# One 128-token tile of experts 1 to 7: w1's 128x128 chunks are held in TensorE and the tokens stream, where the tokens were held and w1 streamed

## The chip, the core and the metric

The kernel runs on one core of one Trainium2 chip. The metric is the time of one execution on the device in microseconds (us), taken as the median of several runs. TensorE (PE) multiplies: it loads a stationary operand of up to 128x128 (rows PEld in the trace) and streams a moving operand through it into PSUM. VectorE (DVE), ScalarE (ACT) and GpSimd (POOL) do the elementwise work; SyncE (SP) and POOL issue transfers.

## The reference, cut to what matters

Three stages follow one another: a block-causal attention over 4 x 8 heads of 576 positions, a dense feed-forward layer with a leaky ReLU, and a mixture of 8 experts. The change touches the last stage alone, and there the experts 1 to 7:

```python
def _moe2_ref(x, w_skip, w_gate, w1, w2):      # x: 2304 x 512, w1: 8 x 512 x 1024, w2: 8 x 1024 x 512
    do_compute = x @ w_skip > 0
    xc = x[do_compute]
    logits = xc @ w_gate
    e_idx = np.argmax(logits, axis=1)
    ...
    for e in range(E):
        mask = e_idx == e
        h = np.maximum(xc[mask] @ w1[e], 0.0)
        y[mask] = gate_w[mask, None] * (h @ w2[e])
    out[do_compute] = xc + y
```

## The kernel before, in words

Attention and the dense layer take the first 700 us or so. Routing then writes, for each expert, a list of its tokens. An expert works through its tokens in tiles of 128: a gather by index brings 128 rows of x, `turn_x` turns them on TensorE so that the 512 features lie on the partitions (four chunks of 128 features x 128 tokens, `xw`), and the tile function does the two products. Expert 0 uses `expert_tile`, which splits each operand in two parts and is not touched. Experts 1 to 7 use `expert_tile32`, in plain fp32; the trace shows each plain fp32 matmul as two records (two passes), each with a weight load of its own, and each transpose as one.

A tile of `expert_tile32` does this. `mm1(f, c)` makes the intermediate values of half f (512 of the 1024 columns) from feature chunk c: the tokens are the stationary operand, 512 columns of w1 move, and the result `ph[f]` has tokens on the partitions. `relu` copies it through ACT into `hs`. The second product needs the intermediate values with their own index on the partitions, so `turn_h` turns `hs` in four 128x128 transposes on TensorE, and DVE copies the result from PSUM into `hw`. `mm2(f)` then multiplies chunk f of `hw` with chunk f of w2 into `py`, eight chunks in a row. Late in the tile `ahead` puts in the `turn_x` of the next expert's first tile. At the end `finish` weighs `py` by the gate and adds x (DVE, L987), and POOL scatters the rows to the output (L988).

The order on TensorE is the order in which the code is written: each matmul is kept in program order. After an expert's first tile stands a branch (the `tc.If` at L1150): all engines read the count of the expert's tokens and jump over the code of the second to fourth tile and of a loop for more, if the count doesn't ask for them. In the names of the trace, `cv` is `xw`, `wbt` and `xT` are the buffers that hold w1 and w2, `raw` is `hw`, `pt` is a PSUM bank of transposes, `xg` and `xgf` are gathered rows, and q behind an engine's name is its sequencer. An expert's weights are loaded by SP (L847, L849) into one of four places, four experts ahead (expert 3's and 4's after expert 0).

Of the kernel before, what the change touches and what calls it, by code (L numbers as in the profile page):

```python
# [15 lines left out]
AF = mybir.ActivationFunctionType  # L16
# [9 lines left out]
def run_all(steps):  # L26
    for s in steps:
        s()
# [318 lines left out]
def attention_moe_kernel(  # L347
# [13 lines left out]
    nc = tc.nc  # L361
# [9 lines left out]
    ND = D // 128  # L371
    NF2 = F2 // 128
# [8 lines left out]
    ident = C.tile([128, 128], F32, name="ident")  # L381
# [535 lines left out]
    def places(own=False):  # L917

        bank = lambda nm, *shape: ps3.tile([128, *shape], F32, name=nm, tag="ps")
        return dict(hh=M3.tile([128, NF2, 128], F32R, name="hh", bufs=1),  # L920
                    hl=M3.tile([128, NF2, 128], F32R, name="hl", bufs=1),
                    ph=[bank("ph3", 512) for _ in range(2)],
                    py=psx.tile([128, 512], F32, name="py", bufs=1) if own else bank("py", 512),
                    pt=lambda: bank("pt", 4, 128), hs=lambda f: M3.tile([128, 512], F32, name="hs"),
                    yo=lambda: M3.tile([128, 512], F32, name="yo"))
# [58 lines left out]
    def finisher(lx, at, py):  # L984
        def finish():
            yo = at["yo"]()
            end = nc.vector.scalar_tensor_tensor(out=yo, in0=py, scalar=lx["li"][:, 2:3], in1=lx["xg"], op0=ALU.mult, op1=ALU.add)  # L987
            nc.gpsimd.indirect_dma_start(out=out[:, :], out_offset=bass.IndirectOffsetOnAxis(ap=lx["ix"][:, 1:2], axis=0),  # L988
                                         in_=yo, in_offset=None, bounds_check=NT - 1, oob_is_err=False)
            return end  # L990

        return finish

    def expert_tile32(e, hw, lx, ahead=(), at=None):

        a, b = weights[e]
        at = at or places()
        ph, py = at["ph"], at["py"]
        h = {}

        def mm1(f, c):
            tc.keep_in_program_order(nc.tensor.matmul(ph[f], lx["xw"][:, c], a[c][:, f * 512 : f * 512 + 512], start=(c == 0), stop=(c == ND - 1)))

        def mm2(f):
            tc.keep_in_program_order(nc.tensor.matmul(py, hw[:, f], b[f], start=(f == 0), stop=(f == NF2 - 1)))

        def relu(f):
            h[f] = at["hs"](f)
            nc.scalar.activation(out=h[f], in_=ph[f], func=AF.Relu)

        def turn_h(f):
            pt = at["pt"]()
            for c in range(4):
                tc.keep_in_program_order(nc.tensor.transpose(pt[:, c], h[f][:, c * 128 : (c + 1) * 128], ident))
            nc.vector.tensor_copy(hw[:, 4 * f : 4 * f + 4], pt)

        for c in range(ND):
            mm1(0, c)
        relu(0)
        for c in range(2):  # L1020
            mm1(1, c)
        turn_h(0)
        for c in range(2, ND):
            mm1(1, c)
        relu(1)
        for f in range(2):
            mm2(f)
        turn_h(1)
        for f in range(2, 6):
            mm2(f)  # L1030
        run_all(ahead)
        for f in range(6, NF2):
            mm2(f)
        return finisher(lx, at, py)
# [6 lines left out]
    for i in range(len(seq) + lag):  # L1041
# [11 lines left out]
        f = i - (len(seq) - NFB)  # L1053
# [16 lines left out]
        if i >= lag:  # L1070
            n, f = seq[i - lag]
# [54 lines left out]
    hw = [CV.tile([128, NF2, 128], F32, name="raw", bufs=3) for _ in range(2)]  # L1126
# [3 lines left out]
    for e in range(E):  # L1130
        ahead1 = [lambda: turn_x(firsts[e + 1])] if e + 1 < E else []
        some = ExitStack()
        if e:
            if e == E - 1:
                some.enter_context(tc.If(nreg[e] > 0))
            second = lane32(lall[1], e, xgs[4], xws[2])
            gather(second)
            finish = expert_tile32(e, hw[0], firsts[e], ahead1, at=places(True))

        def later(k_):  # L1140
# [3 lines left out]
            return (lane32 if e else lane)(L, n, xgs[4 + (k_ + 1) % 2], (xws if e else xts)[2 + (k_ + 1) % 2])  # L1144

        tile_of = (lambda *a: expert_tile32(e, hw[1], *a)) if e else expert_tile

        def more(k_, lx):
# [63 lines left out]
```

## Time and profile before

| | |
|---|---|
| median of 3 runs | 866.15 us (863.11 to 866.83) |
| the profiled execution | 863.9 us, span of the trace 862.1 us |
| PE busy | 795.8 us, 92% of the span |
| DVE, ACT, POOL busy | 518.6, 397.6, 352.3 us |
| experts 1 to 7 | from 739.8 us to the end |

The trace is of one execution; the span runs from its first instruction to its last. In a row of the timeline the first number is the start, the second how long the row lasts, and x12 says that twelve instructions are merged in it; behind it stands in brackets how long the engine had been idle and what it waited for. A matmul's record reaches past the start of the next one, since matmuls are pipelined, so a pace is read from starts.

### The profile page before, as it was taken

The page shows a single profiled execution, that of the slowest core. Times are in us where ns is not written, and L with a number is a line of the kernel's source. Part 1 is how long each engine was busy: PE and PEld are TensorE (multiplying, and loading weights), DVE is VectorE, ACT ScalarE, POOL GpSimd, SP SyncE. Part 2 cuts the span into 40 slices and gives each one's busy share as a digit, 9 for nine tenths or more (in the row PEclk, how much of TensorE's full clock was granted, in tenths as well). Part 3 has the DMA queues.
Part 4 walks back from the last instruction along what each step waited for, and adds up shares of the span by engine and source line. Part 5 has one row for each costly group of instructions (what it writes and reads, how often), then busy time and mean ns, then how long its engine had stood idle before and what let it go on. Part 6 is the DMA issues. An engine that isn't in the chain of part 4 may idle for free. (4 is left out here: it accounts for less than half of the span.)

```text
span 862.1 us, 12392 instructions
## 1 busy us (share of the span) xinstructions
PE 795.8 (92%) x4100; PEld 651.2 (76%) x4100; DVE 518.6 (60%) x1131; ACT 397.6 (46%) x909; POOL 352.3 (41%) x427
## 2 busy tenths in 40 slices
PE   6788999999999989799999999999999969989995
PEld 4577787989889788588999988798998758544442
DVE  6886788888878794776522799977222722111111
ACT  5887788887878774654422212222233312101010
POOL 3765554463545664654323234354225331010210
PEclk9799999999999999999999999999999989999998
DMA  6664753474332152652400663123126651693910
GB/s 164 173 169 100 203 108 94 102 202 118 77 100 56 39 183 82 217 198 74 147 1 16 205 184 110 36 76 111 65 103 207 236 85 37 240 396 134 326 60 7
DMA packets 114653, 112.89 MB, mean 131 GB/s; under 512 B 76718, under 2 KB 79790, under 8 KB 114562
## 3 DMA queue, kind: packets, MB, share of 16 engines
q1 hardware_dynamic: 106386, 95.72, 36.7%
q0 software_dynamic: 8176, 16.06, 6.2%
q8 instruction: 44, 0.72, 0.3%
q14 instruction: 47, 0.39, 0.1%
HBM read 81.23 MB, written 22.70 MB: 121 GB/s over the span
## 5 line engine op out<-in xcount | busy, mean ns | idle before, releaser
L447 PE MATMUL ph<-xT,wbt 128*128 128x384 f32 x864 | 166.8, 338 | 5.0 <-DVE u L438 2.7
L447 PEld LDWEIGHTS ph<-xT,wbt 128*128 128x128 f32 x864 | 152.0, 188 | 14.8 <-DVE u L438 5.0
L439 POOL TENSOR_TENSOR gl<-u,gh 128x384 fp32r<-128x384 f32 x72 | 79.7, 1107 | 155.2 <-ACT gh L438 147.2
L447 PE MATMUL acc<-wbt,gh 128*128 128x512 f32 x432 | 132.9, 396 | 0.0
L185 POOL TENSOR_SCALAR P<-P,stat 128x128 f32<-128x128 f32 (+2 forms) x144 | 79.1, 572 | 76.1 <-DVE stat L183 52.8
L438 DVE TENSOR_TENSOR u<-ph,u 128x384 f32<-128x384 f32 x72 | 39.7, 551 | 89.7 <-ACT u L437 89.7
L438 ACT CAST gh<-u 128x384 fp32r<-128x384 f32 x72 | 36.9, 513 | 121.0 <-DVE u L438 52.7
L447 PEld LDWEIGHTS acc<-wbt,gh 128*128 128x128 f32 x432 | 79.8, 188 | 12.3
L447 PE MATMUL acc<-wbt,gl 128*128 128x512 f32 x216 | 81.9, 395 | 0.0
L285 PE MATMUL pv<-ph,vs 128*128 128x320 f32 (+4 forms) x280 | 70.7, 323 | 2.7 <-DVE ph L239 1.6
L236 PE MATMUL pt<-ident,P 128*128 128x128 f32 x400 | 62.7, 283 | 6.7 <-ACT P L174 2.5
L437 ACT ACTIVATE u<-ph 128x384 f32<-128x384 f32 x72 | 35.2, 489 | 70.6 <-PE ph L447 66.8
L161 PE MATMUL sp<-wbt 128*128 128x128 f32 (+2 forms) x192 | 57.1, 376 | 9.6 <-DVE ph L239 2.8
L447 PE MATMUL ph<-xT,wia 128*128 128x384 f32 x288 | 59.0, 351 | 2.8 <-DVE cv L438 2.0
L447 PE MATMUL po<-woa,gA 128*128 128x512 f32 x216 | 56.2, 403 | 3.5 <-ACT gA L438 2.8
L285 PEld LDWEIGHTS pv<-ph,vs 128*128 128x128 f32 x280 | 51.3, 193 | 9.1 <-DVE ph L239 2.7
L418 POOL TENSOR_TENSOR cv<-cv,cv 128x512 int32<-128x512 int32 x32 | 43.7, 1367 | 33.8 <-DVE cv L417 21.7
L236 PEld LDWEIGHTS pt<-ident,P 128*128 128x128 f32 x400 | 47.1, 144 | 12.8 <-ACT P L174 3.0
L662 DVE CUSTOM_DVE_ANT_0 xlast<-x,raw 128x512 f32<-128x512 f32 x72 | 55.0, 803 | 0.0
L447 PEld LDWEIGHTS ph<-xT,wia 128*128 128x128 f32 x288 | 51.5, 195 | 4.3 <-DVE cv L438 2.5
L243 DVE TENSOR_TENSOR pl<-pt,ph 128x512 fp32r<-128x512 f32 (+2 forms) x84 | 50.9, 624 | 5.1 <-ACT ph L242 4.1
L447 PEld LDWEIGHTS po<-woa,gA 128*128 128x128 f32 x216 | 39.9, 191 | 13.1 <-ACT gA L438 3.7
(244 smaller groups left out, 1533.9 us busy)
## 6 DMA issues: line engine op xcount, KB each, us to landing
wbt<-in_moe_w_dram SPq DMA_DIRECT2D x48, 512.0 KB, 7.7
wbt<-wbt SPq DMA_DIRECT2D x60, 144.0 KB, 2.6
raw<-in_moe_w_in_dram SPq DMA_DIRECT2D x16, 512.0 KB, 4.1
raw<-in_moe_w_out_dram SPq DMA_DIRECT2D x16, 512.0 KB, 4.1
xTd<-xT POOLq DMA_DIRECT2D x4, 1152.0 KB, 8.0
part_d<-cv SPq DMA_DIRECT2D x18, 256.0 KB, 2.1
x<-part_d SPq DMA_DIRECT2D x6, 768.0 KB, 7.9
xT<-xTd POOLq DMA_DIRECT2D x6, 768.0 KB, 7.4
```

What stands on the lines that cost most here:

```text
L161: nc.tensor.matmul(o_, st()[a][h][:, rows : rows + m], st()[b][:, h, c : c + w], start=(i == 0), stop=(i == 1))
L185: nc.gpsimd.tensor_scalar(out=P, in0=P, scalar1=rs[:, i : i + 1], scalar2=1.0, op0=ALU.mult, op1=ALU.mult)
L236: nc.tensor.transpose(o, src, self.ident)
L243: nc.vector.tensor_tensor(out=dl, in0=s_, in1=dh.bitcast(F32), op=ALU.subtract)
L285: nc.tensor.matmul(box["pv"][:, c0:N], v, box[t][:, i, h, cs], start=(jc == 0 and t == "ph"), stop=(jc == runs[-1][0] and t == parts[-1]))
L418: nc.gpsimd.tensor_tensor(out=w, in0=w, in1=low, op=ALU.add)
L437: nc.scalar.activation(out=u, in_=ph, func=AF.Copy, scale=0.01)
L438: return [nc.vector.tensor_tensor(out=u, in0=ph, in1=u, op=ALU.max), nc.scalar.copy(gh, u), nc.gpsimd.tensor_tensor(out=gl, in0=u, in1=gh. ...
L439: nc.gpsimd.tensor_tensor(out=gl, in0=u, in1=gh.bitcast(F32), op=ALU.subtract)]
L447: nc.tensor.matmul(ps, x, y, start=first and m == 0, stop=last and m == 3 * n - 1)
L662: nc.vector.tensor_tensor_reduce(out=junk, in0=x2[:, t], in1=wrow[j], scale=1.0, scalar=0.0, op0=ALU.mult, op1=ALU.add, accum_out=box["L"] ...
```

## The change

The first product of a tile changes sides. The stationary operand is now a 128x128 chunk of w1 (feature chunk c, columns f*128 to f*128+127), and the 128 tokens of `xw` move. `mm1(f)` does four such matmuls for each of eight f, and leaves 128 intermediate values on the partitions and the tokens along the row; four f share one PSUM bank. `relu(i)` writes a whole bank into `hw` at once. `turn_h`, its transposes, the copies by DVE and the tile `hs` are gone. `mm2`, `ahead` and `finish` are as before.

```diff
-        def mm1(f, c):
-            tc.keep_in_program_order(nc.tensor.matmul(ph[f], lx["xw"][:, c], a[c][:, f * 512 : f * 512 + 512], start=(c == 0), stop=(c == ND - 1)))
+        def mm1(f):
+            for c in range(ND):
+                tc.keep_in_program_order(nc.tensor.matmul(
+                    ph[f // 4][:, f % 4 * 128 : f % 4 * 128 + 128], a[c][:, f * 128 : f * 128 + 128], lx["xw"][:, c],
+                    start=(c == 0), stop=(c == ND - 1)))
...
-        def relu(f):
-            h[f] = at["hs"](f)
-            nc.scalar.activation(out=h[f], in_=ph[f], func=AF.Relu)
-
-        def turn_h(f):
-            pt = at["pt"]()
-            for c in range(4):
-                tc.keep_in_program_order(nc.tensor.transpose(pt[:, c], h[f][:, c * 128 : (c + 1) * 128], ident))
-            nc.vector.tensor_copy(hw[:, 4 * f : 4 * f + 4], pt)
+        def relu(i):
+            nc.scalar.activation(out=hw[:, 4 * i : 4 * i + 4].rearrange("p f t -> p (f t)"), in_=ph[i], func=AF.Relu)
 
-        for c in range(ND):
-            mm1(0, c)
+        for f in range(4):
+            mm1(f)
         relu(0)
-        for c in range(2):
-            mm1(1, c)
-        turn_h(0)
-        for c in range(2, ND):
-            mm1(1, c)
+        for f in range(4, NF2):
+            mm1(f)
         relu(1)
-        for f in range(2):
-            mm2(f)
-        turn_h(1)
-        for f in range(2, 6):
+        for f in range(6):
             mm2(f)
         run_all(ahead)
```

On TensorE the code of a tile becomes this (expert 1's second tile stands for all; a row's xN counts matmuls as written, two passes each in fp32, one for a transpose):

```order
 L903 MATMUL pt<-ident,xgf_4228 128x128 x4
-L1002 MATMUL ph_7954<-wbt_7457,cv_7495 128x512 x4
-L1002 MATMUL ph_7955<-wbt_7457,cv_7495 128x512 x2
-L1014 MATMUL pt<-ident,hs 128x128 x4
-L1002 MATMUL ph_7955<-wbt_7457,cv_7495 128x512 x2
-L1005 MATMUL py<-wbt_7458,raw 128x512 x2
-L1014 MATMUL pt<-ident,hs 128x128 x4
-L1005 MATMUL py<-wbt_7458,raw 128x512 x4
+L1006 MATMUL ph_7964<-cv_7495,wbt_7457 128x128 x16
+L1006 MATMUL ph_7965<-cv_7495,wbt_7457 128x128 x16
+L1011 MATMUL py<-wbt_7458,raw 128x512 x6
 L903 MATMUL pt<-ident,xg_7488 128x128 x4
```

The eight transposes of L1014 are gone, and the eight matmuls of 512 columns have become 32 of 128; the first six of `mm2` follow without a break.

On DVE, at the same tile, the two copies of L1015 are gone and nothing takes their place; what stands around them keeps its order (L1143 is the branch that was L1150):

```order
-L1150 COMPARE_AND_BRANCH
-L906 COPY cv_7495<-pt 128x256
-L1015 COPY raw<-pt 128x512 x2
+L1143 COMPARE_AND_BRANCH
+L906 COPY cv_7495<-pt 128x256
 L906 COPY cv_7496<-pt 128x256
 L987 SCALAR_TENSOR_TENSOR yo<-py,la1li,xgf_4228 128x512
```

What moved on DVE is thus only the place of the branch in the queue, by two instructions. ACT keeps two activations in each tile, which now write `raw` and not `hs`. Ahead of expert 1 no engine's order changes.

## Rows read from the trace of the kernel before

**Rows 1.** The page: span, and granted clock in 40 slices.

```profile
span 862.1 us, 12392 instructions
...
PEclk9799999999999999999999999999999989999998
```

**Rows 2.** Busy time by window: two tiles (start:end, length, engines, clock, DMA, GB/s).

```profile
739.50:756.00 16.50, 15.29 (x44) 7.17 (x44) 3.01 (x5) 1.57 (x3) 2.00 (x2) 1.00 0.96 352
...
820.20:835.80 15.60, 15.30 (x45) 7.17 (x44) 2.56 (x4) 1.57 (x3) 1.96 (x2) 1.00 0.10 33
```

**Rows 3.** Timeline of PE, one whole tile (expert 5's) and the next one's start.

```profile
820.57 5.39 PE L1002 MATMUL ph<-wbt,cv 128*128 128x512 f32 x12 [0.30 <-PEq L1150]
825.80 0.60 PE L1014 MATMUL pt<-ident,hs 128*128 128x128 f32 x4
826.23 1.88 PE L1002 MATMUL ph<-wbt,cv 128*128 128x512 f32 x4
827.95 1.88 PE L1005 MATMUL py<-wbt,raw 128*128 128x512 f32 x4
829.67 0.60 PE L1014 MATMUL pt<-ident,hs 128*128 128x128 f32 x4
830.11 3.60 PE L1005 MATMUL py<-wbt,raw 128*128 128x512 f32 x8
833.54 0.60 PE L903 MATMUL pt<-ident,xg 128*128 128x128 f32 x4
833.98 1.88 PE L1005 MATMUL py<-wbt,raw 128*128 128x512 f32 x4
836.16 0.67 PE L1002 MATMUL ph<-wbt,cv 128*128 128x512 f32 x1 [0.30 <-PEq L1150]
```

**Rows 4.** Timeline of PE: the starts of the second and the fourth tile.

```profile
756.94 5.39 PE L1002 MATMUL ph<-wbt,cv 128*128 128x512 f32 x12 [1.84 <-PEq L1150]
...
789.40 5.39 PE L1002 MATMUL ph<-wbt,cv 128*128 128x512 f32 x12 [0.95 <-DVEq L1150]
```

**Rows 5.** Timeline of ACT and DVE in the tile of rows 3.

```profile
828.21 0.60 ACT L1009 ACTIVATE hs<-ph 128x512 f32<-128x512 f32 x1 [3.27 <-PE ph L1002]
...
830.30 0.69 DVE L1015 COPY raw<-pt 128x512 f32<-128x512 f32 x1 [3.18 <-PE pt L1014]
```

**Rows 6.** Timeline of PEld: fp32 loads, for 128 moving columns (attention) and for 9 (routing).

```profile
49.54 0.52 PEld L285 LDWEIGHTS pv<-ph,vs 128*128 128x128 f32 x4
49.98 0.19 PEld L161 LDWEIGHTS sp<-wbt 128*128 128x128 f32 x1
...
676.05 2.65 PEld L678 LDWEIGHTS lt<-wg,xlast 128*128 128x128 f32 x23
678.62 0.30 PEld L915 LDWEIGHTS eph<-wbt,xtf 128*128 128x128 f32 x2
```

**Rows 7.** Timeline of PE: the matmuls that belong to the first loads of rows 6.

```profile
49.55 0.71 PE L285 MATMUL pv<-ph,vs 128*128 128x128 f32 x4
50.01 0.42 PE L161 MATMUL sp<-wbt 128*128 128x384 f32 x1
```

**Rows 8.** Groups by form: one weight load of mm1 and of a transpose (busy, mean ns).

```profile
L1002 PEld LDWEIGHTS ph<-wbt,cv 128*128 128x128 f32 x96 | 17.3, 190 | 25.6 <-issue 24.9 <-ACT cv L905 0.7
...
L1014 PEld LDWEIGHTS pt<-ident,hs 128*128 128x128 f32 x56 | 7.0, 141 | 7.4 <-issue 7.1 <-ACT hs L1009 0.2
```

**Rows 9.** Timeline of SP: the loads of expert 6's weights.

```profile
788.57 1.76 SPq L847 DMA_DIRECT2D wbt<-in_moe_w_dram  x4
790.44 2.25 SPq L849 DMA_DIRECT2D wbt<-in_moe_w_dram  x4
```

**Rows 10.** Transfers from 739 us on: issues, KB each, median us from issue to landing.

```profile
wbt<-in_moe_w_dram SPq DMA_DIRECT2D x32, 512.0 KB, 8.3
```

**Rows 11.** Timeline behind the last tile: the weighing, and the scatter to the output.

```profile
851.49 0.75 DVE L987 SCALAR_TENSOR_TENSOR yo<-py,la0li,xg 128x512 f32<-128x512 f32 x1 [0.89 <-PE py L1005]
852.52 1.00 POOL L988 DMA_INDIRECT out_dram<-yo,la0ix  x1 [13.99 <-DVEq L1180]
```

More of the change, by code (lines that the diff above doesn't have):

```diff
@@ L998, in expert_tile32 @@
         ph, py = at["ph"], at["py"]
-        h = {}
-        def mm1(f, c):
-            tc.keep_in_program_order(nc.tensor.matmul(ph[f], lx["xw"][:, c], a[c][:, f * 512 : f * 512 + 512], start=(c == 0), stop=(c == ND - 1)))
+        def mm1(f):
[3 more added lines that the diff above has]
+                    start=(c == 0), stop=(c == ND - 1)))
         def mm2(f):
             tc.keep_in_program_order(nc.tensor.matmul(py, hw[:, f], b[f], start=(f == 0), stop=(f == NF2 - 1)))
-        def relu(f):
-            h[f] = at["hs"](f)
-            nc.scalar.activation(out=h[f], in_=ph[f], func=AF.Relu)
-        def turn_h(f):
-            pt = at["pt"]()
-            for c in range(4):
-                tc.keep_in_program_order(nc.tensor.transpose(pt[:, c], h[f][:, c * 128 : (c + 1) * 128], ident))
-            nc.vector.tensor_copy(hw[:, 4 * f : 4 * f + 4], pt)
-        for c in range(ND):
-            mm1(0, c)
-        relu(0)
-        for c in range(2):
-            mm1(1, c)
-        turn_h(0)
-        for c in range(2, ND):
-            mm1(1, c)
+        def relu(i):
+            nc.scalar.activation(out=hw[:, 4 * i : 4 * i + 4].rearrange("p f t -> p (f t)"), in_=ph[i], func=AF.Relu)
+        for f in range(4):
+            mm1(f)
+        relu(0)
+        for f in range(4, NF2):
+            mm1(f)
         relu(1)
-        for f in range(2):
-            mm2(f)
-        turn_h(1)
-        for f in range(2, 6):
+        for f in range(6):
             mm2(f)
```

## The prediction

> **What bounds the kernel now.** I read the page first. The span is 862.1 us and the clock row stands at 9 in nearly every slice, full speed, 2.4 GHz [rows 1]; the change touches only what comes after 739.8 us, so the next view was busy time by window there. In the window of expert 5's tile PE is busy 15.30 us of 15.60 at granted clock 1.00, while DVE has 2.56 us, ACT 1.57 and the DMA share is 0.10 [rows 2]. So in this stage TensorE alone sets the time, and whatever is taken from PE's own queue comes off the end. The timeline of PE then gives a tile piece by piece [rows 3]: three quarters of mm1 from 820.57, four transposes at 825.80, the rest of mm1, four passes of mm2, four transposes at 829.67, and so on; the next tile starts at 836.16, 15.59 us later. No PE row inside the tile has an idle time in brackets, so no wait inside it is there to be removed: the change can only gain what the transposes cost as work.
>
> The number of tiles comes from the groups: 56 loads of transposes of hs, eight in a tile, make seven tiles in this execution [rows 8].
>
> **What goes.** Eight transposes in each tile. In rows 3 four take from 825.80 to 826.23 and from 829.67 to 830.11, 0.43 and 0.44 us, so 0.87 us a tile and 6.1 us in seven tiles. DVE's copies (0.69 us each, [rows 5]) and the tile hs go too; they lay beside PE's work and are worth nothing by themselves.
>
> **What is added.** mm1 has the same number of multiplications but another form. Before: 16 passes of 512 columns; a pass takes (833.54 - 830.11)/8 = 0.429 us [rows 3], so 6.86 us. After: 64 passes of 128 columns, each with a weight load of its own. The streaming alone is a quarter of 0.429, 0.107 us, and would cost nothing more. The question is the load, for there are 64 now instead of 16. Before, a load (190 ns in its record, [rows 8]) lay behind 0.429 us of streaming; that cover is gone.
>
> The trace has this very shape elsewhere. In attention four fp32 loads for 128 moving columns start at 49.54 and the next one at 49.98 [rows 6]: 0.44/4 = 0.110 us for load and pass together. The matmuls that belong to them start at 49.55 and the next one at 50.01 [rows 7]: 0.115 us, the first one's start included. In the routing 23 fp32 loads for only 9 moving columns start at 676.05 and the next load at 678.62 [rows 6]: 2.57/23 = 0.112 us. With 9 columns there is hardly any streaming, so 0.112 us is the load itself; with 128 columns, 0.107 us of streaming, it is no slower. Load and stream lie beside each other, and the slower one, the load, sets the pace. I take 0.112 us, the longest series: 64 x 0.112 = 7.17 us, against 6.86 before, so 0.31 us more a tile.
>
> The Trainium skill speaks against the change here: "TensorE: Matmul & The Clock Gate", Part 3, section "The mechanism", says that a weight load overlaps matmuls in flight only when it goes to another group of rows of the array. All loads here fill all rows. By the row a pass costs 0.112 us; by that rule it would cost load and stream one after the other (a rival below). The two series just read, 9 and 128 columns at one pace, contradict it for fp32.
>
> **The sum.** Removed 0.87, added 0.31: 0.56 us a tile. Seven tiles give 3.9 us. The bounds of the pace: as low as 0.107 us if the load hid wholly behind the stream (then the 0.87 is kept nearly whole, 6.1 us in seven tiles), as high as the 0.115 us of rows 7 (64 x 0.115 = 7.36, 0.37 a tile, 2.6 us). Nearest is the long fp32 series, since each load here also follows another fp32 load without a break.
>
> **Waits that could come.** mm2(0) needs relu(0), which now writes hw itself. relu takes 0.60 us and used to start 0.26 us after mm1's last pass gave way to mm2 at 827.95 [rows 3, 5]; between the end of f = 3 and mm2(0) stand 32 passes of mm1, 3.6 us, so about 2.7 us are to spare. mm2(4) needs relu(1); behind mm1 come eight passes of mm2, 8 x 0.429 = 3.4 us, against 0.9. If that cover were gone, each of the two would cost its 0.9 us, and the gain would turn into a loss; nothing in the order takes it away. Weights: SP issues expert 6's last four loads at 790.44 to 792.69 [rows 9], they land 8.3 us after issue in the median [rows 10], and the tile that needs them starts at 836.16 [rows 3]. A stage that is 4 us shorter doesn't reach that. Behind the last tile DVE weighs from 851.49 and POOL scatters at 852.52 [rows 11]; that follows the last matmul as before and moves forward with it.
>
> The profiled execution took 863.9 us, 1.8 more than its span, and would take 863.9 - 3.9 = 860.0. The median of the three runs is 866.15, 2.25 above it; from the median I predict **862.2 us**, a ratio of 0.9955. I count 0.5% (4.3 us) as what a measurement of this kernel can tell from no change; the forecast lies just inside of it.
>
> **Rivals.**
> 1. *Less comes through, because code arrives late.* Between tiles PE branches over code that isn't needed. In rows 3 this leaves PE idle for 0.30 us on either side of the tile, put down to its own sequencer [rows 3], but ahead of the second tile it is 1.84 us, and ahead of the fourth 0.95 us, put down to DVE's sequencer [rows 4], in the time when weights stream in at a DMA share of 0.96 [rows 2]. A tile's PE code grows from 44 load-and-matmul pairs (32 passes and 12 transposes) to 84, and the code that is jumped over grows alike. If that wait ends at a moment that DMA traffic sets, a tile that ends 0.56 us earlier just waits longer. For it: the wait is longest where DMA is busiest. Against: that is one wait of this length among the tiles shown, and what PE does just before the branch (transposes of the next tile's tokens and four passes of mm2) doesn't change. Price: the savings of one to three tiles lost (0.6 to 1.7 us), and up to another 1.54 us (1.84 - 0.30) if a short wait becomes a long one: 863 to 865.5 us.
> 2. *More comes through.* Loads hide wholly (0.107 us) or the 1.84 us wait vanishes (1.5 us): 862.2 - 2.2 = 860.0, or 860.7; with both 858.5. For it: transposes of 128 columns run at 0.109 us with a load each [rows 3], but their loads are shorter, 141 ns against 190 [rows 8]. Against it: the 0.112 us of the routing is a load's own time, and mm1's loads have the same 190 ns.
> 3. *The other side: loads don't overlap.* A pass then costs 0.112 + 0.107 = 0.219 us, mm1 14.0 us, the tile 6.3 us more, seven tiles 44 us: 910 us. It decides from a pace of (6.86 + 0.87)/64 = 0.121 us up, where the removed transposes are eaten, and is slower by over 0.5% from 0.130 us. Against it stand rows 6 and 7. By the rule of the Trainium skill named above this is what would happen; the trace disagrees. The operands differ from attention's only in that the stationary one is a slice of a bigger buffer, which the slice of wbt in rows 6's next load also is.
> 4. *The change doesn't do what it says.* The transposes are gone from the order, and nothing else left PE's path, so I see no way for this one.
>
> **Chances.** Forecast (seven tiles at 0.110 to 0.115 us, 861.5 to 863.5): 0.52. Rival 1: 0.26. Rival 2: 0.17. Rival 3 or another loss: 0.05. The line at 0.5% faster is 861.8 us, 0.4 below the forecast: rival 2 lies below it (0.17), and so does about a third of the forecast's own case, 0.18, since a pace of 0.110 us in place of 0.112 already gives 4.8 us and runs differ by a microsecond or two. That makes faster 0.36. Slower (over 870.5) is rival 3's 0.05. The rest, 0.59, is same. The range leaves out the ends of rivals 2 and all of 3 and allows the spread of the runs: 858.5 to 865.5 us.
>
> **What the profile after would show.** PE: no transposes of hs; a row of 64 passes of 128 columns about 7.2 us long, without a break, and starts of fp32 loads 0.110 to 0.112 us apart. Tiles 15.0 us apart where they were 15.59. The pieces of mm2 unchanged at 0.429 us a pass, and no idle time at mm2(0) or mm2(4). DVE has 14 copies of 0.69 us less. What would make it wrong: loads 0.12 us apart or more (rival 3 in part), tiles short as foreseen but longer idle times before the second and fourth tile (rival 1), or a granted clock below 1.00 in this stage, which no row of before leads me to expect.

## The result, and the profile after

| | before | after |
|---|---|---|
| median of 8 runs | 865.77 us (861.0 to 879.22) | 859.99 us (855.25 to 863.61) |
| ratio, 95% interval | | 0.9918 (0.9889 to 0.9947) |
| profiled execution | 863.9 us | 860.66 us |
| span, and from expert 1's first pass to its end | 862.1 us, 122.3 us | 858.9 us, 116.8 us |
| PE, DVE busy | 795.8, 518.6 us | 793.2, 508.2 us |

The kernel is faster by 5.8 us at the medians. The ratio is what the means of all sixteen runs give, which differ by 7.1 us; one run of the kernel before, 879.22 us, lies 12 us above the next, and without it the means differ by 5.3 us (0.9939). The two profiles differ by only 3.2 us, since expert 1 happened to start at 742.08 us in that of after and at 739.81 in that of before, although nothing ahead of it differs. So all that follows compares the stage by itself: from the first pass of expert 1 to the end of the span it takes 5.5 us less.

The page of after: span, busy time of the engines, granted clock in 40 slices, and the queue of instruction code (packets, MB, share of 16 DMA engines).

```profile
span 858.9 us, 12943 instructions
...
PE 793.2 (92%) x4380; PEld 675.7 (79%) x4380; DVE 508.2 (59%) x1117; ACT 397.0 (46%) x909; POOL 351.8 (41%) x427
...
PEclk9899999999999998999999999999999999999998
...
q8 instruction: 48, 0.79, 0.4%
```

Busy time by window in after, the first tile and expert 5's, as in [rows 2]:

```profile
741.80:756.80 15.00, 14.69 (x84) 10.49 (x84) 0.85 (x2) 1.57 (x3) 1.99 (x2) 1.00 0.97 348
818.20:833.20 15.00, 14.69 (x84) 10.50 (x84) 0.77 (x3) 1.57 (x3) 1.96 (x2) 1.00 0.19 52
```

A tile keeps PE busy for 14.69 us, where it was 15.29 and 15.30, at granted clock 1.00 (2.4 GHz) as before. DVE has 0.8 us in it where it had 2.56.

The timeline of PE in after: the starts of the second and the fourth tile (as [rows 4]), then expert 5's tile whole (as [rows 3]).

```profile
757.15 7.38 PE L1006 MATMUL ph<-cv,wbt 128*128 128x128 f32 x64 [0.37 <-PEq L1143]
...
788.07 7.38 PE L1006 MATMUL ph<-cv,wbt 128*128 128x128 f32 x64 [0.55 <-PEq L1143]
...
818.47 7.38 PE L1006 MATMUL ph<-cv,wbt 128*128 128x128 f32 x64 [0.71 <-PEq L1143]
825.69 5.32 PE L1011 MATMUL py<-wbt,raw 128*128 128x512 f32 x12
830.84 0.60 PE L903 MATMUL pt<-ident,xg 128*128 128x128 f32 x4
831.28 1.88 PE L1011 MATMUL py<-wbt,raw 128*128 128x512 f32 x4
833.46 0.79 PE L1006 MATMUL ph<-cv,wbt 128*128 128x128 f32 x5 [0.30 <-PEq L1143]
```

Read the starts. mm1 is one row of 64 passes and lasts 825.69 - 818.47 = 7.22 us. The next tile starts 833.46 - 818.47 = 14.99 us later, and 0.30 us of it is idle, as before; so the tile is 15.59 - 14.99 = 0.60 us shorter. No row inside it has an idle time. The second tile now waits 0.37 us where it waited 1.84, the fourth 0.55 where it waited 0.95, the sixth 0.71 where it was 0.30.

ACT in that tile of after, and behind it the last tile's end (DVE, POOL), as in [rows 5, 11]:

```profile
822.38 0.60 ACT L1014 ACTIVATE raw<-ph 128x512 f32<-128x512 f32 x1 [5.94 <-PE ph L1006]
825.95 0.60 ACT L1014 ACTIVATE raw<-ph 128x512 f32<-128x512 f32 x1 [2.97 <-PE ph L1006]
...
848.19 0.75 DVE L987 SCALAR_TENSOR_TENSOR yo<-py,la0li,xg 128x512 f32<-128x512 f32 x1 [0.89 <-PE py L1011]
849.22 1.00 POOL L988 DMA_INDIRECT out_dram<-yo,la0ix  x1 [13.40 <-DVEq L1173]
```

relu(0) ends at 822.98, 2.71 us before mm2 starts at 825.69: the cover is what the prediction worked out (2.7).

The loads of mm1 in after, grouped by form (count, then busy and mean ns of one), as in [rows 8]:

```profile
L1006 PEld LDWEIGHTS ph<-cv,wbt 128*128 128x128 f32 x384 | 43.3, 192 | 6.9 <-issue 6.2 <-ACT cv L905 0.8
```

The records of the loads last what they did (192 ns against 190); there are four times as many.

**Where the 5.5 us come from.** Seven tiles, each 0.60 us less work, are 4.2 us. The idle time ahead of the seven tiles, read from the brackets of the tiles' first rows, falls from 4.80 to 3.40 us in sum, which is 1.4. Together 5.6. The experiments ask whether the two parts are what they seem, and what that idle time is.

### The profile page after: what moved, and what is told of

It is laid out like the page before. It is cut to its first block, busy times and chain, and to the rows that moved or that the text cites. A ratio compares the mean times of both kernels' runs of the same rounds, so it can differ in the third digit from the quotient of the medians.

```text
span 858.9 us, 12943 instructions
## 1 busy us (share of the span) xinstructions
PE 793.2 (92%) x4380; PEld 675.7 (79%) x4380; DVE 508.2 (59%) x1117; ACT 397.0 (46%) x909; POOL 351.8 (41%) x427
## 5 line engine op out<-in xcount | busy, mean ns | idle before, releaser
L906 DVE COPY cv<-pt 128x256 f32<-128x256 f32 x9 | 3.8, 424 | 88.9 <-ACTq L1143 61.2
```

The source lines that it names most:

```text
L906: nc.vector.tensor_copy(lx["xw"][:, 2:4], pt[:, 2:4])
```

## The experiments

Experiments 1, 3 and 5 and the changed kernel once more (e1, e3, e4, a2) shared one chip and the same 25 runs of the kernel before (median 867.45 us); the others ran on two more chips, with 869.19 (experiments 2 and 6, b2) and 866.2 us (experiments 7 to 9) for the kernel before. The stage is always from expert 1's first pass to the end of the span.

**1. The transposes alone put back.** On the changed kernel eight transposes in each tile, at their old places; nobody reads their result.

```diff
+        def turn_h(i):
+            pt = at["pt"]()
+            for c in range(4):
+                tc.keep_in_program_order(nc.tensor.transpose(pt[:, c], hw[:, 4 * i + c], ident))
...
-        for f in range(4, NF2):
+        for f in range(4, 6):
+            mm1(f)
+        turn_h(0)
+        for f in range(6, NF2):
             mm1(f)
         relu(1)
-        for f in range(6):
+        for f in range(2):
+            mm2(f)
+        turn_h(1)
+        for f in range(2, 6):
             mm2(f)
```

> The changed kernel with the eight transposes a tile put back as dead work: four chunks of hw behind six of mm1's eight f, four behind two chunks of mm2, into a PSUM bank that nobody reads. Theory (the gain is transposes off PE's own queue, less a dearer mm1): each block of four costs 0.43 to 0.44 us again, tiles stand 15.0 + 0.87 = 15.9 us apart, 0.3 us more than the 15.59 before; seven tiles 6.1 us slower than the changed kernel, ratio to the kernel before 0.998 to 1.004. Rival (the gain came from shorter waits at the branches, the transposes lay under something): tiles stay at 15.0 us, ratio 0.99 to 0.995.

Measured: 876.02 us, 1.0124 of before (1.0052 to 1.0196), stage 130.3 us, 13.5 more than the changed kernel's. The timeline of PE: the second tile's start, then a later tile.

```profile
761.30 1.24 PE L1006 MATMUL ph<-cv,wbt 128*128 128x128 f32 x9 [0.52 <-PEq L1154]
766.86 6.22 PE L1006 MATMUL ph<-cv,wbt 128*128 128x128 f32 x39 [4.31 <-issue]
...
833.27 5.60 PE L1006 MATMUL ph<-cv,wbt 128*128 128x128 f32 x48 [0.78 <-DVE yo L987]
838.70 0.60 PE L1019 MATMUL pt<-ident,raw 128*128 128x128 f32 x4
839.14 1.95 PE L1006 MATMUL ph<-cv,wbt 128*128 128x128 f32 x16
...
849.24 1.02 PE L1006 MATMUL ph<-cv,wbt 128*128 128x128 f32 x7 [0.41 <-PEq L1154]
```

Four transposes take 839.14 - 838.70 = 0.44 us, and the tile 849.24 - 833.27 = 15.97, of which 0.41 is idle: 0.87 us more work than in after, as in the prediction's first term. That is 6.1 us in seven tiles. The other seven, which the expectation did not have, are not the transposes: PE stops for 4.31 us after nine passes of the second tile's mm1, and no semaphore is named ("issue"). Busy time by window there (the columns of [rows 2]):

```profile
763.00:765.00 2.00, 0.00 (x0) 0.00 (x0) 0.00 (x0) 0.00 (x0) 1.63 (x2) 1.00 1.04 394
768.00:769.00 1.00, 1.00 (x7) 1.00 (x6) 0.00 (x0) 0.00 (x0) 0.00 (x0) 0.50 1.06 404
```

In the stop only POOL works, and the DMA engines are full (1.04). Behind it the granted clock is 0.50 (1.2 GHz) for some 3 us, so 39 passes take 772.91 - 766.86 = 6.05 us where 39 x 0.113 = 4.40 are their due. The sum: 6.1 + 4.31 + 1.65 + 1.23 (idle ahead of the tiles, 4.63 against 3.40) = 13.3 us, of 13.5.

**2. Passes of 128 columns with the old sides.** On the kernel before, each pass of 512 columns is cut in four; the tokens stay stationary, and the transposes stay.

```diff
-        def mm1(f, c):
-            tc.keep_in_program_order(nc.tensor.matmul(ph[f], lx["xw"][:, c], a[c][:, f * 512 : f * 512 + 512], start=(c == 0), stop=(c == ND - 1)))
+        def mm1(f, s):
+            for c in range(ND):
+                tc.keep_in_program_order(nc.tensor.matmul(
+                    ph[f][:, s * 128 : s * 128 + 128], lx["xw"][:, c], a[c][:, f * 512 + s * 128 : f * 512 + s * 128 + 128],
+                    start=(c == 0), stop=(c == ND - 1)))
```

> The kernel before (tokens held, w1 moving, transposes kept), but w1 moves in pieces of 128 columns and not of 512: 64 weight loads in mm1, the tokens loaded again for each. Theory (the price of the change is the number of loads, whichever operand is held): a pass 0.112 us as in the changed kernel, mm1 7.17 us for 6.86, tiles 15.9 us apart where the branch costs 0.30 (15.59 before), ratio 0.999 to 1.006. Rival (it is w1 as the held operand that costs 0.112): passes 0.107 to 0.109 us apart, tiles as before, 15.59 to 15.7.

Measured: 881.18 us, 1.0143 of before (1.0100 to 1.0185; before 869.19 on this chip), stage 134.8. The timeline of PE:

```profile
761.92 1.35 PE L1003 MATMUL ph<-wbt,cv 128*128 128x128 f32 x10 [1.81 <-PEq L1153]
767.30 7.43 PE L1003 MATMUL ph<-wbt,cv 128*128 128x128 f32 x38 [4.03 <-issue]
774.58 0.60 PE L1017 MATMUL pt<-ident,hs 128*128 128x128 f32 x4
...
836.79 5.60 PE L1003 MATMUL ph<-wbt,cv 128*128 128x128 f32 x48 [1.89 <-PEq L1153]
842.22 0.60 PE L1017 MATMUL pt<-ident,hs 128*128 128x128 f32 x4
...
852.76 5.60 PE L1003 MATMUL ph<-wbt,cv 128*128 128x128 f32 x48 [0.40 <-PEq L1153]
```

48 passes take 842.22 - 836.79 = 5.43 us, 0.113 each, as with the sides changed. The tile's work is 15.97 - 0.40 = 15.57 us against 15.29 before: 0.28 more. So the second term is the price of four times as many loads and has nothing to do with which operand is held. The run is 12 us slower, and as in the first experiment most of it is a stop without a named reason (4.03 us), idle time ahead of tiles, and a slow clock behind the stop (774.58 - 767.30 = 7.28 us for 38 passes, where 4.29 are due); the tiles' work explains 7 x 0.28 = 2.0 us.

**3. What waits for the late relu.** On the changed kernel mm2 takes the second half's chunks first, so that it needs relu(1) at once.

```diff
-        def mm2(f):
-            tc.keep_in_program_order(nc.tensor.matmul(py, hw[:, f], b[f], start=(f == 0), stop=(f == NF2 - 1)))
+        def mm2(i):
+            f = (i + 4) % NF2
+            tc.keep_in_program_order(nc.tensor.matmul(py, hw[:, f], b[f], start=(i == 0), stop=(i == NF2 - 1)))
```

> The changed kernel, but mm2 starts with the chunks of the second half (4 to 7) and takes the first half after them: same work, only the cover of the second relu is gone. Theory: mm2 now waits for relu(1), 0.26 us to its start and 0.60 us for itself, so PE idles 0.8 to 0.9 us ahead of mm2 in each tile, tiles 15.9 us apart, 6 us slower than the changed kernel, ratio to the kernel before 0.997 to 1.004. Rival (there is slack elsewhere, such as the branch or the next tile's tokens, that takes it up): less than 0.3 us a tile, ratio about 0.99 to 0.994.

Measured: 872.99 us, 1.0063 of before (1.0026 to 1.0100), stage 126.5. The timeline of PE:

```profile
828.65 7.38 PE L1006 MATMUL ph<-cv,wbt 128*128 128x128 f32 x64 [3.15 <-SPq L1174]
836.78 5.42 PE L1012 MATMUL py<-wbt,raw 128*128 128x512 f32 x12 [0.75 <-ACT raw L1015]
...
844.76 1.47 PE L1006 MATMUL ph<-cv,wbt 128*128 128x128 f32 x11 [0.40 <-PEq L1144]
```

From mm1's start to mm2's 8.13 us pass where 7.22 did, and the tile's work grows by 1.0 us (16.11 - 0.40 against 14.99 - 0.30). So the cover of relu(1) that the prediction named is real, and without it a tile costs what it said (0.9) and a tenth more; the cover of relu(0) was not taken away in any run and rests on the 2.71 us read above. That is 7 of the 9.7 us by which the stage grew. Most of the rest is the wait of 3.15 us ahead of this tile.

**4. The same two kernels again.** No edit.

> The changed kernel once more, for its time beside the others and for a second set of idle times ahead of the tiles. Theory: tiles 14.99 us apart where the branch costs 0.30 us, ratio to the kernel before 0.989 to 0.995 (four us of work, up to 1.5 us of branch waits, and the spread of the runs); the idle times ahead of the tiles that differed from before (0.37 where 1.84 was, 0.55 for 0.95, 0.71 for 0.30) come out differently again. Rival (the change itself shortened the branches): 0.37, 0.55 and 0.71 us repeat.

> The kernel before, unchanged, for a second set of PE's idle times ahead of its tiles (first set: 0.65, 1.84, 0.46, 0.95, 0.30, 0.30, 0.30 us). Theory (code for the branch's far side comes through the same transfers as the weights, so the wait depends on where the code lies in its 16 KB pieces and on the traffic): the 1.84 us repeats to within some tenths, as the same code lies in the same place. Rival (pure chance): between 0.30 and 0.6 us this time.

The changed kernel: 861.56 us, 0.9945 (0.9914 to 0.9976), idle ahead of its tiles 3.77 us in sum, stage 117.0. The kernel before, one execution with a profile: 872.51 us, stage 125.0. Its second tile's start:

```profile
763.25 7.08 PE L1002 MATMUL ph<-wbt,cv 128*128 128x512 f32 x12 [2.28 <-PEq L1150]
```

The long wait ahead of the second tile is there again, 2.28 us, and here the granted clock behind it is 0.50, so that 12 passes last 7.08 us where [rows 4] have 5.39. It belongs to the kernel before and not to one execution. The changed kernel has 0.37 us at that place both times, and 0.55 ahead of the fourth tile, against the expectation that they would come out differently; only the sixth's went from 0.71 to 0.99.

**5. More code that is jumped over.** On the changed kernel the third and fourth tile of an expert, which are never entered here, get mm1 three times over.

```diff
+        for _ in range(again):
+            for f in range(NF2):
+                mm1(f)
...
-                    finish = tile_of(lx, ahead + (ahead1 if filled else []))
+                    finish = tile_of(lx, ahead + (ahead1 if filled else []), **(dict(again=2) if e and k_ > 1 else {}))
```

> The changed kernel, but in the code of an expert's third and fourth tile, which no expert from 1 to 7 enters with these tokens, mm1 stands three times: 128 matmuls more that are jumped over by each branch. Theory (the jump's price does not hang on the distance): PE's idle time ahead of the tiles stays at 0.30 to 0.71 us, ratio to the kernel before as for the changed kernel, 0.989 to 0.995. Rival (code that arrives late): idle times of about 1.8 us ahead of most tiles, 5 us or more slower than the changed kernel, ratio about 0.998 or above.

Measured: 861.40 us, 0.9944 (0.9911 to 0.9977), the changed kernel's time. Ahead of the second tile it waits 0.30 us; ahead of the sixth it is 1.43, more than was expected. The rival's 1.8 us ahead of most tiles did not come, so how much code a branch jumps over does not set the wait.

**6. Code put in another place.** In both kernels 32 transposes more stand in expert 0's loop for further tiles, which is never entered; that moves PE's code of experts 1 to 7 back by 32 loads and 32 transposes, and that of ACT and DVE by eight copies each.

```diff
-                        turn_x(lx)
+                        for _ in range(1 if e else 9):
+                            turn_x(lx)
```

> The kernel before with 32 more transposes (and their copies) in the code of expert 0's loop for a fifth and later tiles, which is never entered: about 4 KB more of PE code ahead of expert 1, nothing else. Theory (place of the code): the pattern of idle times ahead of the tiles changes, the 1.84 us goes or moves to another tile; tiles stay 15.59 us apart where the wait is 0.30. Rival (the wait belongs to the tile's own work): again 1.84 ahead of the second tile and 0.95 ahead of the fourth.

> The changed kernel with the same 4 KB of unused PE code ahead of expert 1. Theory (place of the code): idle times differ from 0.65, 0.37, 0.52, 0.55, 0.30, 0.71, 0.30 us, and a stop inside mm1 such as the 4.31 us of the kernel with transposes put back may appear in the tiles at 740 to 770 us, where weights stream in. Rival (the change shortened the waits by its own order): 0.37 and 0.55 us again, no stop inside mm1.

Measured in one execution each, before at 869.19 us: 873.58 us for the kernel before (stage 127.0; the wait ahead of the second tile stays long, 2.10 us, and those ahead of the fifth and sixth grow from 0.30 to 1.65 and 1.38) and 869.21 us for the changed one (stage 122.6, 5.6 to 5.8 more than without the shift). The timeline of PE in the shifted kernel before, fifth tile, and in the shifted changed one:

```profile
813.27 5.39 PE L1002 MATMUL ph<-xT,cv 128*128 128x512 f32 x12 [1.65 <-PEq L1150]
...
759.90 2.02 PE L1006 MATMUL ph<-cv,wbt 128*128 128x128 f32 x16 [0.49 <-PEq L1143]
765.36 7.14 PE L1006 MATMUL ph<-cv,wbt 128*128 128x128 f32 x48 [3.44 <-issue]
772.34 5.32 PE L1011 MATMUL py<-wbt,raw 128*128 128x512 f32 x12
```

Nothing that is executed differs, yet PE now stops for 3.44 us after 16 passes of the second tile, and the 48 passes behind it take 6.98 us where 5.4 are due. So where the code lies decides whether the changed kernel has such a stop; in the kernel before the same shift lengthened waits at branches and made no stop. Shifted alike, the two stages still differ by 127.0 - 122.6 = 4.4 us, about what the tiles' work is worth (4.2).

**7. The same without the weights' traffic.** Experts 4 to 7 use the weights of 1 to 3, and their loads are left out: on the kernel before, and on the shifted changed one.

```diff
+        if e > 3:
+            weights[e] = weights[1 + (e - 1) % 3]
+            return
```

> The kernel before, but the weights of experts 4 to 7 are never loaded; those experts multiply with weights of experts 1 to 3, so the output is another. From 750 us on the transfers are nearly quiet. Theory (weights hold up the code): ahead of the second tile 0.3 to 0.5 us in place of 1.84 and 2.28, no fall of the granted clock there; tiles 15.59 us apart. Rival (the wait has nothing to do with the weights): 1.8 us or more again.

> The changed kernel with the 4 KB of unused code ahead of expert 1, which stopped for 3.44 us inside mm1 of the second tile, but without the loads of experts 4 to 7's weights (they multiply with weights of experts 1 to 3; the output is another). Theory (weights hold up the code): no stop inside mm1, the second tile's mm1 is 7.2 us long, tiles 15.0 us apart. Rival (the shifted code itself stops there): 3 us or more again.

One execution each: 862.42 us (stage 121.2) and 863.87 us (stage 117.3, where the shift alone gave 122.6). The kernel before waits 0.68 us ahead of its second tile where it waited 1.84 and 2.28; 0.3 to 0.5 was expected. The shifted one, timeline of PE:

```profile
759.54 2.02 PE L1009 MATMUL ph<-cv,wbt 128*128 128x128 f32 x16 [0.30 <-PEq L1146]
762.40 5.52 PE L1009 MATMUL ph<-cv,wbt 128*128 128x128 f32 x48 [0.83 <-issue]
767.75 5.32 PE L1014 MATMUL py<-wbt,raw 128*128 128x512 f32 x12
```

It stops after the same 16 passes, for 0.83 us where the theory had no stop and the rival 3 or more, and the 48 passes behind it take 767.75 - 762.40 = 5.35 us, full speed. The place is the code's; the length shrinks with the traffic.

**What ends these stops.** The trace records the transfers of instruction code as two queues of their own: packets of 16 KB, 44 of them in the kernel before and 48 in the changed one, and packets of 8 KB, 47 and 45. PE's code is what grew, so I read the first queue as PE's. The view of DMA for a tenth of a microsecond shows one packet, and from its share (of 16 engines' time) how long it took. Experiment 1, from 764.2 to 764.3 us:

```profile
q8 instruction: 1, 0.02, 70.4%
```

The shifted changed kernel, from 762.9 to 763.0:

```profile
q8 instruction: 1, 0.02, 68.8%
```

And that without the weights' traffic, from 759.6 to 759.7:

```profile
q8 instruction: 1, 0.02, 84.6%
```

The first took 0.704 x 16 x 0.1 = 1.13 us; it began at 764.25 and landed at 765.38, in the middle of the stop, and PE went on 1.48 us later. The same reading for all the stops, and for all waits of 0.68 us or more ahead of the second to the seventh tile that the trace puts down to PE's own sequencer:

| kernel, place | code packet begins, lands | PE goes on | behind the landing |
|---|---|---|---|
| before, 2nd tile | 754.09, 755.18 | 756.94 | 1.76 |
| before again, 2nd tile | 760.47, 761.56 | 763.25 | 1.69 |
| before, shifted, 2nd tile | 759.37, 760.47 | 762.18 | 1.71 |
| before, shifted, 5th tile | 810.48, 811.53 | 813.27 | 1.74 |
| before, fewer weights, 2nd tile | 752.64, 753.74 | 755.41 | 1.67 |
| old sides, 2nd tile | 759.12, 760.19 | 761.92 | 1.73 |
| old sides, 6th tile | 833.78, 834.90 | 836.79 | 1.89 |
| after, 6th tile | 815.79, 816.74 | 818.47 | 1.73 |
| after again, 6th tile | 812.90, 813.87 | 815.61 | 1.74 |
| more code jumped over, 6th tile | 816.68, 817.63 | 819.36 | 1.73 |
| weights later, 6th tile | 821.03, 821.98 | 823.71 | 1.73 |
| after, shifted, 6th tile | 823.98, 824.96 | 826.64 | 1.68 |
| transposes back, inside mm1 | 764.25, 765.38 | 766.86 | 1.48 |
| old sides, inside mm1 | 764.96, 766.09 | 767.30 | 1.21 |
| after, shifted, inside mm1 | 762.90, 764.00 | 765.36 | 1.36 |
| the same, fewer weights | 759.68, 761.03 | 762.40 | 1.37 |
| for comparison: after, 2nd tile (0.37 us idle) | 754.07, 755.12 | 757.15 | 2.03 |

Behind a branch PE starts 1.67 to 1.76 us after a block of code has landed, in eleven rows of twelve (the other is 1.89); inside mm1 1.2 to 1.5 us after. These waits end with code. A packet itself takes no longer under the traffic (1.07 to 1.13 us in the rows of the second tile, against 1.10 and 1.35 with fewer weights); what comes late is its beginning. Shorter waits don't show it so clearly, and not every wait is one: the fourth tile's 0.95 us in the kernel before, put down to DVE's sequencer [rows 4], ends 3.5 us behind the last block's landing. In the last row the code is there in time, and only the branch itself is left, 0.37 us. The 3.15 us of experiment 3, put down to SP's sequencer, also end 1.32 us after a packet's landing (826.35 + 0.98 = 827.33, and 828.65), which is one case only. And the next block comes later under the traffic: at a DMA share of 1.0 two blocks begin 5.7 to 6.4 us apart (754.09 and 759.76 before; 764.25 and 770.64 in experiment 1), with fewer weights 2.6 to 3.2 (752.64 and 755.80 at a share of 0.12; 753.85, 756.45 and 759.68 at 0.70).

On this the Trainium skill, "Runtime: NRT & Kernel Launch", section "Instruction fetch mechanics", says that a taken branch out of the window of code forces a fetch before execution goes on, and that crossing from one 16 KiB block to the next is "mostly hidden". The waits at the branches fit the first (up to 2.28 us, ended by a packet), though no row shows that it was the branch that asked for the block; the stops of 3.44 to 4.31 us inside mm1 are not hidden. All of them lie 1.2 to 2.0 us behind the start of a tile that a branch has jumped to, so whether straight code far from a branch can stop in this way is not shown.

**8. Can the traffic be moved out of the way?** On the changed kernel an expert's weights are loaded one expert later.

```diff
-            load_expert(e + 4)
+            load_expert(e + 3)
         else:
             load_expert(3)
-            load_expert(4)
```

> The changed kernel with each expert's weights loaded three experts ahead and not four: after expert 0 only expert 3's, after expert 1 expert 4's, and so on. A try at a better version: between 740 and 755 half the traffic. Theory (traffic at the branch costs): idle times ahead of the second and fourth tile no longer than 0.3 to 0.4 us, at best 1 us less than the changed kernel, ratio to the kernel before 0.987 to 0.994. Rival: weights now come late for some tile, PE waits on a transfer for a microsecond or more, ratio above 0.995.

Measured: 863.25 us, 0.9947 (0.9916 to 0.9977), stage 116.8, as the changed kernel. Its idle times are the same to 0.1 us (0.30, 0.62 and 0.72 ahead of the second, fourth and sixth tile). But the traffic did not move. The third group of loads on SP in the changed kernel, then in this run, and the first 30 us of the stage in each (the columns of [rows 2]):

```profile
745.82 5.12 SPq L847 DMA_DIRECT2D xT<-in_moe_w_dram  x4
...
751.28 4.93 SPq L847 DMA_DIRECT2D xT<-in_moe_w_dram  x4
...
742.08:772.08 30.00, 29.62 (x172) 21.46 (x172) 1.74 (x4) 3.13 (x6) 5.90 (x6) 1.00 1.01 379
...
747.33:777.33 30.00, 29.70 (x172) 21.46 (x172) 1.74 (x4) 3.13 (x6) 5.90 (x6) 1.00 1.01 378
```

SP starts that group 3.74 us after expert 1's first pass in the one and 3.95 in the other, and the DMA share is 1.01 in both: the issue was moved in the code and hardly in time. So this run does not say whether lighter traffic would save anything in the changed kernel.

**9. Expert 0 in the same way.** On the changed kernel expert 0, whose operands are split in two parts, changes sides too: 96 passes of 128 columns for a tile's half, no transposes.

```diff
-        m1 = [products(ph[f], lx["xT"], [(a[0][c][:, fs[f]], a[1][c][:, fs[f]]) for c in range(ND)]) for f in range(2)]
+        piece = lambda f: products(ph[f // 4][:, f % 4 * 128 : f % 4 * 128 + 128], [(a[0][c][:, f * 128 : f * 128 + 128], a[1][c][:, f * 128 : f * 128 + 128]) for c in range(ND)], lx["xT"])
+        m1 = [[x for f in range(4 * i, 4 * i + 4) for x in piece(f)] for i in range(2)]
...
```

> The changed kernel with the same change in expert 0's four tiles: there each product is three fp32r passes, the pieces of w1 become the held operand, 24 passes of 512 columns become 96 of 128, and eight transposes a tile go; ACT and DVE write the two parts of the intermediate values straight from PSUM. Theory (a pass can't be shorter than its weight load, 0.112 us): fp32r streams 512 columns in 0.233 us, 24 of them 5.6 us, but 96 loads take 10.7 us; less 0.87 us of transposes that is 4.3 us more a tile, some 17 us in four tiles: ratio to the kernel before 1.008 to 1.018. Rival (removing transposes pays wherever it is done): another 2 to 4 us faster than the changed kernel, ratio 0.985 to 0.991.

Measured: four executions against 866.2 us before. One took 873.96 us (0.9% more, mean granted clock 0.979), the other three 887.27 to 892.51 (clock 0.961 to 0.966), so no ratio is given. The profile is of the one of 892.51. The timeline of PE, two tiles of expert 0:

```profile
711.19 20.74 PE L915 MATMUL ph<-xtf,wbt 128*128 128x128 f32 x96 [1.44 <-DVE xtf L909]
731.73 1.16 PE L915 MATMUL py<-xT,hh 128*128 128x512 f32 x2
...
739.72 10.83 PE L915 MATMUL ph<-xt,wbt 128*128 128x128 f32 x96
750.38 0.68 PE L915 MATMUL py<-xT,hh 128*128 128x512 f32 x2
...
751.14 0.62 PE L915 MATMUL py<-xT,hh 128*128 128x512 f32 x2
751.61 0.39 PE L915 MATMUL py<-xT,hl 128*128 128x512 f32 x1
```

A pass costs (750.38 - 739.72)/96 = 0.111 us here, the load's pace again, and in the first of the two tiles (731.73 - 711.19)/96 = 0.214. The windows tell why:

```profile
715.00:720.00 5.00, 5.00 (x26) 5.00 (x25) 1.25 (x6) 0.00 (x0) 2.21 (x3) 0.50 0.85 68
...
735.00:739.00 4.00, 4.00 (x23) 3.36 (x22) 0.29 (x1) 0.86 (x2) 0.00 (x0) 1.00 0.00 0
739.00:750.00 11.00, 11.00 (x97) 10.85 (x96) 2.17 (x4) 0.60 (x1) 1.98 (x2) 1.00 0.17 49
```

The granted clock is 0.50 in the first tile and 1.00 in the second; only the second bears on the price of a pass. There a pass of 512 columns takes (751.61 - 751.14)/2 = 0.235 us, so its quarter would stream in some 0.06, an estimate. A new operand's 0.111 is longer, so cutting the pass in four makes the load the bound: 96 passes take 10.66 us where 24 long ones would take 5.6, and the eight transposes saved do not pay for that. What the four tiles cost in sum without the slow clock was not taken apart.

## Why the prediction was right, and where its sizes were off

- **PE alone sets the end of the stage: right.** PE is busy 14.69 of 15.00 us, and the work that experiments 1 to 3 put into the tiles shows in the length of the stage.
- **Removed, 0.87 us a tile: right.** Putting the transposes back costs 0.87.
- **Added, 0.31 us a tile from a pace of 0.112: right, a little too dear.** mm1 takes 7.22 us where 7.17 was foreseen; but the old mm1 took more than its 16 x 0.429 too, 827.95 - 820.57 - 0.43 = 6.95 us [rows 3], since a tile's first twelve passes take 825.80 - 820.57 = 5.23 us where 12 x 0.429 = 5.15. The difference is 0.27, and the tile's gain 0.60 where the sum had 0.56: 4.2 us in place of 3.9. The old sides with short passes gave 0.28 by themselves.
- **Loads that don't overlap (rival 3): ruled out.** 64 loads of full rows run at 0.113 us with 128 columns, 0.112 with 9 [rows 6]. The Trainium skill's rule in "TensorE: Matmul & The Clock Gate", Part 3, "The mechanism", which lets a load overlap only for another group of rows (the same section's words on a background weight buffer aside), would by the estimate have made a tile 6.3 us longer; the trace disagrees.
- **Covers of the relus: right.** No idle time at mm2(0) or mm2(4); without that of relu(1) it costs 1.0 us a tile; that of relu(0) was not tried.
- **The waits ahead of the tiles stay as they are: the mis-sized step.** The sum had them at no change; they fell by 1.4 us (in a2's profile by 1.0 against the first of before, by 1.6 against b2's). Rival 2 named the end of the 1.84 us wait as possible. Rival 1 had the right mechanism, code that arrives late under the weights' traffic, but the wrong sign for this kernel: it took the moment of arrival as fixed. In fact the block came 12.0 us after expert 1's first pass in after (754.07 - 742.08) and 14.3 before (754.09 - 739.81), 2.3 earlier for a tile that is 0.6 shorter. That it came earlier because the code lies elsewhere is argued from experiment 6 and not shown for this wait. With the code shifted, the same change has rival 1's loss, a stage of 122.6 us, as long as the unshifted kernel's before. That this part came out as a gain is luck of the placement. The prediction also put the fourth tile's 0.95 us into the time of full traffic; from 784.0 to 789.4 us the DMA share before is 0.02 and less, so that wait was none of the traffic's.
- **Median.** The median measured, 859.99 us, is 2.2 below the forecast and inside the range. 4.2 us of work and 1.4 of code make 5.6; the ratios of the two comparisons of the changed kernel give 7.1 us (4.6 to 9.6; 5.3 without the run of 879.22) and 4.8 (2.1 to 7.5). The work is thus shown by the tiles' rows, while the code's part in a median is known to a microsecond or two only. The chance given for a gain above 0.5%, 0.36, is 0.35 by its own terms (0.17 and 0.18).

What stays open: what decides the moment at which a block of code is requested, so that one could place code on purpose; why its beginning comes late under full traffic; whether the queue of 16 KB packets serves PE alone; and why expert 1 starts between 738.9 and 747.3 us in profiles whose earlier stages are the same.

## What to carry to other kernels

Cost a short matmul by the pace of its weight load and not by its columns: read that pace from a row of loads with few columns, and turn an operand round where the transposes saved cost more than the loads added (here 0.87 against 0.27 us a tile in plain fp32, but not in expert 0's form, where the load is the slower part by far). When a kernel with much straight code changes by a few microseconds, look at the code queue's packets beside the idle times before crediting the edit: a shift of code that is never run made the changed kernel's stage 5.6 us longer, in one execution. Judge such an edit by the work inside a tile, and by the whole only over more than one placement.

## What was not expected of the hardware

- A load of full rows in plain fp32 hides behind streaming and streaming behind it: 0.112 us a pass at 9 columns [rows 6] and 0.113 at 128, with either operand held.
- Late code can starve PE inside a row of matmuls, 1.2 to 2.0 us behind a branch's target: stops of 3.44, 4.03 and 4.31 us at a DMA share of 1.03 to 1.05, 0.83 us with fewer weights. Blocks of code then begin 5.7 to 6.4 us apart and not 2.6 to 3.2.
- A stop can cost twice: behind those of 2.10, 2.28, 3.44 and 4.31 us the granted clock was 0.50 for some 3 us, and behind that of 4.03 for some 6; in experiment 6 this made 48 passes take 6.98 us and not 5.4. Behind 1.84 us [rows 4], and behind the 3.15 us of experiment 3, it was 1.00.
- In the profiled execution of experiment 9 the clock stayed at 0.50 for a whole row of 96 short passes (20.5 us) though PE was busy throughout (5.00 of 5.00), after an idle time of 1.44 us; it was 1.00 again from 735 us, some 3 us after the 512-column passes had begun at 731.73.
